# Four early blocks instead of two pass layer one twice: a quarter of its tiles first, the rest later

## The chip, the cores and the metric

The kernel runs on one core of a Trainium2 chip. The metric is the device time in microseconds of one execution. The engines are TensorE (PE), VectorE (DVE), ScalarE (ACT), GpSimdE (POOL) and SyncE (SP), which here issues every DMA.

## The reference

Attention over 4 batches, 8 heads, 576 positions and 64 columns a head, causal, with a linear memory beside it; then two dense layers over the 4 x 576 = 2304 rows of 512 columns:

```python
scores = scale * q @ k.T                      # causal, softmax
local = softmax(scores) @ v
q_p = elu(q) + 1
mem_out = (q_p @ M_prev) / (q_p @ z_prev + 1e-6)
x = sigmoid(beta) * mem_out + (1 - sigmoid(beta)) * local     # heads side by side: 2304 x 512
h = x @ w_in;  x = leaky_relu(h, 0.01) @ w_out                # layer one, 512 -> 2048 -> 512
h = x @ w_in2; out = (h - tanh(h)) @ w_out2                   # layer two
```

All values are float32. The kernel gets near float32 in the dense layers by splitting each operand into a high and a low part and adding three products (high x high, high x low, low x high).

## The kernel before

**Units and blocks.** A unit is one head pair of one batch. An A unit holds the first 256 queries and 256 keys; a B unit holds the other 320 queries (three query tiles) and all 576 keys. There are 16 A units (batch by batch, four head pairs each), then 16 B units. Four units make a block of 256 rows: blocks 0 to 3 from A, 4 to 7 from B; block 8 is gathered from the last 64 queries of each batch. A unit's steps (class Unit): load q, k, v and the memory (L444 to L481); the memory part, which takes phi of the raw queries and divides it by its norm on DVE and ACT (L490 to L531); its transposes (L539); the scores (L576, L581), masked and searched for their maximum on DVE (L602), exponentials on ACT (L622), scaling (L639, L641); transposes of the exponentials (L695), copied to SBUF (L397 and its neighbours); then memory and values into one PSUM tile o (L662, L717), and the copy of o into the block's x (fin, L730).

**Weights.** A weight arrives as the two 32-bit words of a 64-bit number. convert makes float32 of them and then the two parts: an absolute value on ACT (c_abs, L770), four steps on DVE (L773, L776, L781, L786), the high part (usually ACT, L393) and the low part (usually DVE, L406). Layer one has 32 such tiles of 128 x 512, 16 of either matrix. A pair p needs four of them. Layer two's weights are converted in 64 chunks, stored to DRAM, and loaded over layer one's when those are done with.

**Layer one.** layer1(n, p0, p1) passes block n over pairs p0 to p1 - 1, a sweep. It splits x into high and low halves (xs), does 24 up matmuls a pair (L835), the leaky ReLU (L892), the split of its result g, and 24 down matmuls a pair (L915) into two PSUM tiles dn. A sweep over part of the pairs stores dn as a partial sum (xps), and the later sweep loads it and adds it (L936). The order of the sweeps is SWEEPS (L387): blocks 0 and 1 over pairs 0 to 3, blocks 0 and 1 over pairs 4 to 7, and then blocks 2 to 8 over all eight.

**What sets the order.** The class Schedule is a planner that runs while the program is built. Each step has a priority, the engines it may go to with a time for each, the steps it needs and the buffers it takes. At every point of its own clock each free engine takes the first step by priority that is ready by the planner's times and has its buffers; the steps then stand in that fixed order in the engine's queue on the chip. Attention has priority (0, unit + offset), with offsets -1 for scores, 0 for loads, 0.3 for the memory part and 0.6 for values. A layer-one tile i has (0, 3.2 + 0.02 i) for the first 16 and (0, 7.2 + 0.02 i) for the rest. ACT, DVE and SP steps of layer one have (-1, n), ahead of everything; its matmuls have (1, ...), behind attention. RINGS (L33) gives the number of buffers of each tile; a ring's buffer comes free when all that use it are done. The two buffers of x hold a block's attention output until its last sweep has split it.

**Layer two** (L1093 to L1119) is written out by hand and follows when the planned part has ended.

Of the kernel before, what the change touches and what calls it, by code (L numbers as in the profile page):

```python
# [9 lines left out]
F32 = mybir.dt.float32  # L10
# [22 lines left out]
RINGS = {  # L33
# [3 lines left out]
}  # L37
# [195 lines left out]

W1_FROM, W1_STEP = (3.2, 7.2), 0.02

SPLIT = 2
W2_FROM, W2_STEP = 14, 0.25
# [3 lines left out]
def kernel(  # L241
# [42 lines left out]
    mask = const.tile([128, 512], BF16, name="mask")  # L284
    mask4 = const.tile([128, S], BF16, name="mask4")
    omg4 = const.tile([128, H // 2], F32, name="omg4")
# [20 lines left out]
    )  # L307
    nc.gpsimd.memset(mask4[:, 0:512], 0.0)
    for i in range(2):
        nc.vector.tensor_copy(out=mask4[64 * i:64 * i + 64, 512:S], in_=mask[0:64, 384:448])  # L310
    for m in mbs:
# [49 lines left out]

    x2s = [dram.tile([128, KT, 256], F32, name=f"x2s{n}") for n in range(NBLK)]
    xps = [dram.tile([128, KT, 256], F32, name=f"xps{n}") for n in range(SPLIT)]
    x8s = dram.tile([128, KT, 256], F32, name="x8s")
# [18 lines left out]
    x8_h = sc.new(None)  # L383
    x2_h = [sc.new(None) for n in range(NBLK)]
    xp_h = [[sc.new(None) for i in range(2)] for n in range(NBLK)]

    SWEEPS = [(n, h * NP // 2, (h + 1) * NP // 2) for h in range(2) for n in range(SPLIT)]  # L387
    SWEEPS += [(n, 0, NP) for n in range(SPLIT, NBLK)]
# [22 lines left out]
    class Unit:  # L411
# [14 lines left out]
        def declare(self, pr, prev):  # L426
            kind, b, hp = self.kind, self.b, self.hp
            nq, nk, nqc, nkc, q0 = self.nq, self.nk, self.nqc, self.nkc, self.q0
            n, nf = nqc + nkc, nq * 128
            op = lambda *a, **kw: sc.op(*a, prio=(pr[0], pr[1] + OFFSET[part_]), **kw)  # L430
            part_ = "load"
            new = sc.new
# [6 lines left out]

            qk, rq, zb, mb, v_ = new("qk"), new("rq"), new("zb"), new("mb"), new("v")  # L440
            n0 = 0 if kind == "A" else NA
# [25 lines left out]
            def load_v(e):  # L467
                v_.tile = att.tile([128, 2, 5, 64], F32, name="v", bufs=RINGS["v"])
                if kind == "B":
                    nc.sync.dma_start(  # L470
                        out=v_.tile, in_=v[b, 2 * hp:2 * hp + 2].rearrange("h (t p) d -> p h t d", p=128))
                    return
                for i, h in enumerate(heads):
                    nc.sync.dma_start(
                        out=v_.tile[:, i, 0:nk, :],
                        in_=v[b, h, 0:nk * 128, :].rearrange("(t p) d -> p t d", p=128))
# [68 lines left out]
            order["p"] = op([("pe", nq * 109 + 50)], tr_p, reads=[ph], alloc=[s, pT], after=in_order("p"))  # L545
            op(copies(nqc, True), p_out, reads=[s], writes=[pT], port=False)

# [5 lines left out]
            for tiles in ([[0, 1]] if kind == "A" else [[2], [3], [4]]):  # L553
                ss = [new("s"), new("s")]
                c0 = 0
                for t in tiles:
                    nn = min(S, (t + 1) * 128)
                    et[t - q0] = new(f"e{t if t > 1 else t + 2}")
                    made[t] = (ss, new("mx"), c0)
                    c0 += nn  # L560
# [27 lines left out]
            for i in range(nq):  # L588
# [7 lines left out]
                def maxi(e, j, t=t, ss=ss, ei=ei, mx=mx, nn=nn, half=half, c0=c0):  # L596
                    if t < 4:
                        out, in0, in1 = ei.tile[:, j, :], ss[j].tile[:, c0:c0 + nn], mask[:, 512 - nn:512]
                    else:
                        c = slice(j * half, (j + 1) * half)  # L600
                        out, in0, in1 = ei.tile[:, c], ss[j].tile[:, 0:half], mask4[:, c]
                    nc.vector.tensor_tensor_reduce(  # L602
                        out=out, in0=in0, in1=in1, scale=-scale,
                        scalar=mx.tile[:, 0:1] if t == 4 and j else BIG, op0=ALU.add, op1=ALU.min,
                        accum_out=mx.tile[:, j:j + 1])
# [7 lines left out]
                for j in range(2):  # L613
                    op([("dve", DVE(width))], lambda e, j=j, f=maxi: f(e, j), port=False,
                       reads=[ss[j]] + ([mx] if t == 4 and j else []), writes=[ei, mx])
# [51 lines left out]
            for kt in range(nk):  # L667
# [42 lines left out]
                for j in range(len(ss)):  # L710
                    op(copies(2 * w if len(ss) == 1 else w, True), lambda e, j=j, f=e_out: f(e, j), port=False,
                       reads=[ss[j]], writes=[pt])
# [17 lines left out]
            def fin(e):  # L730
                if xh.tile is None:
                    xh.tile = x_p.tile([128, KT, 320], F32, name="x")
                copy(e, xh.tile[:, hp, 0:nqc], o.tile[:, 0:nqc])

            op(copies(nqc, True), fin, reads=[o], writes=[xh], alloc=[xh] if first_x else [], port=False)
            if kind == "B":

                def rest(e):
                    nc.sync.dma_start(
                        out=x8s[:, hp, b * REST:(b + 1) * REST], in_=xh.tile[:, hp, 256:320])  # L740

                op([("sp", 500)], rest, reads=[xh], writes=[x8_h], lat=2300)

# [98 lines left out]
    def layer1(n, p0, p1):  # L842

        kind, b = blocks[n]
        sop = lambda *a, **kw: sc.op(*a, prio=(-1, n), **kw)
        if kind == "R":
            x = sc.new("x")

            def load_x(e):
                x.tile = x_p.tile([128, KT, 320], F32, name="x")  # L850
                nc.sync.dma_start(out=x.tile[:, :, 0:NA], in_=x8s)

            sop([("sp", 600)], load_x, reads=[x8_h], alloc=[x], lat=2600)
        else:
            x = x_h[kind, b]
        xs = sc.new("xs")

        def x_hi(e, i):
            if xs.tile is None:
                xs.tile = xs_p.tile([128, 2, KT, 256], F32R, name="xs")  # L860
            copy(e, xs.tile[:, 0, 2 * i:2 * i + 2], x.tile[:, 2 * i:2 * i + 2, 0:256])

        def x_lo(e, i):
            low(e, xs.tile[:, 1, 2 * i:2 * i + 2], x.tile[:, 2 * i:2 * i + 2, 0:256],
                xs.tile.bitcast(F32)[:, 0, 2 * i:2 * i + 2])

        for i in range(2):
            sop([("act", ACT(512)), ("dve", DVE(256))], lambda e, i=i: x_hi(e, i), reads=[x] + [xs] * i,
                writes=[xs], alloc=[] if i else [xs])
            sop([("dve", DVE(512))], lambda e, i=i: x_lo(e, i), reads=[x, xs], writes=[xs])  # L870
        dn = [sc.new("dn0"), sc.new("dn1")]
# [92 lines left out]
    for i, (m, f) in enumerate((m, f) for p in range(NP) for m in range(2) for f in (2 * p, 2 * p + 1)):  # L964
        firsts.append(convert(m, f, 0, 0, (0, W1_FROM[i // (2 * NP)] + i * W1_STEP), firsts[i - AHEAD:i - AHEAD + 1] if i >= AHEAD else ()))
    for i, (m, f, c) in enumerate(chunks):
# [197 lines left out]
```

## Time and profile before

| | us |
|---|---|
| median of 3 runs | 1095.72 (1094.59 to 1097.95) |
| profiled execution | 1094.87 |
| its span, first to last instruction | 1093.1 |
| PE busy | 1047.4 (96%) |
| DVE busy | 753.0 (69%) |
| ACT busy | 640.0 (59%) |
| POOL busy | 101.1 (9%) |

PE, DVE, ACT and POOL work side by side, so the busy times are not added. A PE row's end is modelled, and one row reaches into the next; the distance between the starts of two rows is the time that the first took. The granted clock is the share of TensorE's full rate. Times in a timeline are microseconds from the start of the span.

### The profile page before, as it was taken

The page shows a single profiled execution, that of the slowest core. Times are in us where ns is not written, and L with a number is a line of the kernel's source. Part 1 is how long each engine was busy: PE and PEld are TensorE (multiplying, and loading weights), DVE is VectorE, ACT ScalarE, POOL GpSimd, SP SyncE. Part 2 cuts the span into 40 slices and gives each one's busy share as a digit, 9 for nine tenths or more (in the row PEclk, how much of TensorE's full clock was granted, in tenths as well). Part 3 has the DMA queues.
Part 4 walks back from the last instruction along what each step waited for, and adds up shares of the span by engine and source line. Part 5 has one row for each costly group of instructions (what it writes and reads, how often), then busy time and mean ns, then how long its engine had stood idle before and what let it go on. Part 6 is the DMA issues. An engine that isn't in the chain of part 4 may idle for free.

```text
span 1093.1 us, 20334 instructions
## 1 busy us (share of the span) xinstructions
PE 1047.4 (96%) x7488; PEld 920.1 (84%) x7488; DVE 753.0 (69%) x2029; ACT 640.0 (59%) x1348; POOL 101.1 (9%) x103
## 2 busy tenths in 40 slices
PE   4796999999999999999999999999999999999997
PEld 2493987777887887788999999999999999999996
DVE  6999977878658748845222156777777777777774
ACT  5868576767547638635111023776667666676664
POOL 0000000000000000000000000122222222222221
PEclk8597899999999999999999999999999999999999
DMA  7857045656436426425000025201101101010000
GB/s 236 243 163 224 15 109 147 177 156 178 129 86 188 143 74 181 140 53 166 6 34 20 1 83 188 79 1 40 39 1 39 38 3 39 1 39 20 1 20 20
DMA packets 113906, 96.22 MB, mean 88 GB/s; under 512 B 63504, under 2 KB 92688, under 8 KB 113808
## 3 DMA queue, kind: packets, MB, share of 16 engines
q1 hardware_dynamic: 113808, 94.93, 29.5%
q8 instruction: 59, 0.97, 0.4%
q14 instruction: 39, 0.32, 0.1%
HBM read 75.50 MB, written 19.40 MB: 87 GB/s over the span
## 4 chain that ended last, share of the span: by engine, by line
PE 81%; DVE 7%; DMA 4%; ACT 4%; issue 1%; SPq 1%; ACTq 0%; DVEq 0%
PE up L835 34%; PE dn L1081 18%; PE dn L915 16%; PE s L695 4%; PE o L717 3%; PE s L576 3%; DMA w<-in_moe_w_out_dram 2%; DMA cv<-in_moe_w_in_dram 1%; PE o L662 1%; ACT e L622 1%; PE s L581 1%; DVE e L602 1%; DVE cv L786 1%; DVE w L406 1%; DVE cv L781 1%
## 5 line engine op out<-in xcount | busy, mean ns | idle before, releaser
L835 PE MATMUL up<-xs,w 128*128 128x256 f32 x3456 | 447.2, 284 | 2.1 <-ACT xs L393 1.1
L835 PEld LDWEIGHTS up<-xs,w 128*128 128x128 f32 x3456 | 431.1, 192 | 13.7 <-issue 5.8
L915 PE MATMUL dn<-gh,w 128*128 128x256 f32 x1152 | 161.3, 287 | 0.0
L915 PEld LDWEIGHTS dn<-gh,w 128*128 128x128 f32 x1152 | 146.5, 192 | 6.4 <-issue 5.7
L1081 PE MATMUL dn<-w,gh 128*128 128x512 f32 x576 | 144.2, 393 | 1.4 <-ACT gh L1068 1.3
L1058 DVE SCALAR_TENSOR_TENSOR gf<-u,w 128x512 f32<-128x512 f32 x72 | 86.3, 1199 | 81.9 <-ACT w L1055 81.9
L406 POOL TENSOR_TENSOR gl<-gf,gh 128x512 fp32r<-128x512 f32 x72 | 93.7, 1301 | 502.0 <-ACT gh L1068 502.0
L892 ACT ACTIVATE g<-up 128x512 f32<-128x512 f32 x72 | 42.7, 593 | 162.5 <-PE up L835 160.4
L1081 PEld LDWEIGHTS dn<-w,gh 128*128 128x128 f32 x576 | 103.3, 188 | 20.6 <-ACT gh L1068 2.1
L1050 ACT ACTIVATE u<-up 128x512 f32<-128x512 f32 x72 | 43.0, 597 | 116.3 <-PE up L835 116.3
L622 ACT ACTIVATE e<-e,mx 128x128 f32<-128x128 f32 (+4 forms) x144 | 82.6, 576 | 13.9 <-DVE mx L602 9.2
L395 DVE CAST gh<-g 128x512 fp32r<-128x512 f32 x39 | 16.7, 427 | 106.0 <-ACT g L892 105.9
L915 PE MATMUL dn<-gl,w 128*128 128x256 f32 x576 | 83.7, 286 | 0.0
L695 PE MATMUL s<-identr,e 128*128 128x128 f32 x448 | 68.3, 293 | 11.6 <-ACT e L639 5.0
L915 PEld LDWEIGHTS dn<-gl,w 128*128 128x128 f32 x576 | 74.9, 192 | 4.1 <-issue 3.9
L1081 PE MATMUL dn<-w,gl 128*128 128x512 f32 x288 | 77.0, 390 | 0.0
L695 PEld LDWEIGHTS s<-identr,e 128*128 128x128 f32 x448 | 52.6, 148 | 23.1 <-ACT e L639 8.2
L602 DVE CUSTOM_DVE_ANT_0 e<-s,mask 128x128 f32<-128x128 f32 (+4 forms) x144 | 64.0, 483 | 11.3 <-PE s L576 10.3
L393 ACT ACTIVATE pt<-s 128x320 f32<-128x320 f32 (+4 forms) x148 | 57.9, 437 | 18.9 <-PE s L683 12.8
L1081 PEld LDWEIGHTS dn<-w,gl 128*128 128x128 f32 x288 | 54.1, 188 | 11.2
L576 PE MATMUL s<-qk 64*128 64x128 f32 (+3 forms) x256 | 56.0, 524 | 5.3 <-DMA qk<-in_qkt_dram 4.5
L1061 DVE COPY_PREDICATED gf<-mk,up 128x512 f32<-128x512 int32 x72 | 53.7, 746 | 7.8 <-DVE up L1060 0.5
(92 smaller groups left out, 1316.5 us busy)
## 6 DMA issues: line engine op xcount, KB each, us to landing
w<-in_moe_w_in_dram SPq DMA_DIRECT2D x16, 512.0 KB, 5.2
w<-in_moe_w_out_dram SPq DMA_DIRECT2D x16, 512.0 KB, 4.8
cv<-in_moe_w_in_dram SPq DMA_DIRECT2D x32, 256.0 KB, 3.3
vs<-cv SPq DMA_DIRECT2D x64, 128.0 KB, 2.0
cv<-in_moe_w_out_dram SPq DMA_DIRECT2D x32, 256.0 KB, 3.1
v<-vs SPq DMA_DIRECT2D x32, 256.0 KB, 3.2
qk<-in_qkt_dram SPq DMA_DIRECT2D x16, 448.0 KB, 3.6
v<-in_v_dram SPq DMA_DIRECT2D x16, 320.0 KB, 3.4
```

The costliest lines, as they stand in the source:

```text
L393: nc.scalar.activation(out=out, in_=in_, func=AF.Copy)
L406: (nc.vector if e == "dve" else nc.gpsimd).tensor_tensor(out=out, in0=in_, in1=high, op=ALU.subtract)
L576: nc.tensor.matmul(ss[j].tile[:, c0:c0 + nn], lhsT=qk.tile[p, a:a + 128], rhs=qk.tile[p, kc:kc + nn], start=True, stop=True)
L602: nc.vector.tensor_tensor_reduce(out=out, in0=in0, in1=in1, scale=-scale, scalar=mx.tile[:, 0:1] if t == 4 and j else BIG, op0=ALU.add, op ...
L622: nc.scalar.activation(out=x, in_=x, func=AF.Exp, scale=-1.0, bias=mx.tile[:, k:k + 1], accum_out=sm.tile[:, j:j + 1])
L695: nc.tensor.transpose(ss[j].tile[:, a:a + 128], x, ident)
L835: nc.tensor.matmul(ps()[:, s, :], lhsT=w[:, wh * 512 + kt * 128:wh * 512 + (kt + 1) * 128], rhs=xs()[:, xh, kt, :], start=(kt == 0 and j = ...
L915: nc.tensor.matmul(dn[m // 2].tile[:, m % 2, :], lhsT=w[:, wh * 512 + m * 128:wh * 512 + (m + 1) * 128], rhs=gg.tile[:, s * 256:(s + 1) * ...
L1050: nc.scalar.activation(out=u, in_=h, func=AF.Square)
L1058: nc.vector.scalar_tensor_tensor(out=g, in0=u, scalar=lin, in1=w, op0=ALU.mult, op1=ALU.add)
L1061: nc.vector.copy_predicated(out=g, mask=mk.bitcast(I32), data=h)
L1081: nc.tensor.matmul(dn[t], lhsT=g[:, c0:c0 + 128], rhs=w[:, wh * 512:(wh + 1) * 512], start=(p == 0 and s == 0 and j == 0), stop=(p == NP - ...
```

## The change

SPLIT goes from 2 to 4, and CUT = 2 is new: blocks 0 to 3 pass pairs 0 and 1, then blocks 0 to 3 pass pairs 2 to 7, then blocks 4 to 8 pass all eight. The first 8 tiles' priority begins at 3.7, that of the other 24 at 15.7, with steps of 0.002. A first sweep stores its x to DRAM (xsv); the second loads it back in two halves, into buffers named e0 and e1. The A units of odd head pairs keep their exponentials in e0 and e1 too, so that two A units have buffers of their own. Raw queries get two buffers instead of one. A and B units' values are separate tiles, two buffers for A and one for B (before: two for both). The conversion of weights (cv) has three buffers instead of four. The x tile has 256 columns instead of 320: a B unit's last 64 columns are copied from o to a tile of their own (xr) and stored from there. Attention's copies out of PSUM and its maxima, which free a PSUM tile, get the priority (-0.5, unit + offset), ahead of every other attention step and of the conversions (free_op). The mask of the last query tile is kept for one half only, and the plain mask serves the other.

```diff
@@ -31,9 +31,9 @@
 RINGS = {
-    "qk": 2, "rq": 1, "zb": 2, "mb": 2, "v": 2, "ph": 1, "dnm": 2, "pT": 1, "mx": 6, "sm": 6,
-    "e2": 1, "e3": 1, "e4": 1, "s": 3, "o": 1, "pt": 4, "x": 2, "xs": 1,
-    "g": 2, "gl": 2, "gh": 2, "up": 2, "dn0": 1, "dn1": 1, "cv": 4, "v2": 4,
+    "qk": 2, "rq": 2, "xr": 1, "zb": 2, "mb": 2, "v": 1, "va": 2, "ph": 1, "dnm": 2, "pT": 1, "mx": 6, "sm": 6,
+    "e0": 1, "e1": 1, "e2": 1, "e3": 1, "e4": 1, "s": 3, "o": 1, "pt": 4, "x": 2, "xs": 1,
+    "g": 2, "gl": 2, "gh": 2, "up": 2, "dn0": 1, "dn1": 1, "cv": 3, "v2": 4,
 }
@@ -231,9 +231,11 @@
-W1_FROM, W1_STEP = (3.2, 7.2), 0.02
-SPLIT = 2
+W1_FROM, W1_STEP = (3.7, 15.7), 0.002
+SPLIT = 4
+CUT = 2
 W2_FROM, W2_STEP = 14, 0.25
@@ -282,7 +284,7 @@
     mask = const.tile([128, 512], BF16, name="mask")
-    mask4 = const.tile([128, S], BF16, name="mask4")
+    mask4 = const.tile([128, S // 2], BF16, name="mask4")
     omg4 = const.tile([128, H // 2], F32, name="omg4")
@@ -305,9 +307,9 @@
     )
-    nc.gpsimd.memset(mask4[:, 0:512], 0.0)
+    nc.gpsimd.memset(mask4[:, 0:S // 2 - 64], 0.0)
     for i in range(2):
-        nc.vector.tensor_copy(out=mask4[64 * i:64 * i + 64, 512:S], in_=mask[0:64, 384:448])
+        nc.vector.tensor_copy(out=mask4[64 * i:64 * i + 64, S // 2 - 64:S // 2], in_=mask[0:64, 384:448])
     for m in mbs:
@@ -360,6 +362,7 @@
     x2s = [dram.tile([128, KT, 256], F32, name=f"x2s{n}") for n in range(NBLK)]
+    xsv = [dram.tile([128, KT, 256], F32, name=f"xsv{n}") for n in range(SPLIT)]
     xps = [dram.tile([128, KT, 256], F32, name=f"xps{n}") for n in range(SPLIT)]
@@ -382,9 +385,10 @@
     x2_h = [sc.new(None) for n in range(NBLK)]
+    xv_h = [sc.new(None) for n in range(NBLK)]
     xp_h = [[sc.new(None) for i in range(2)] for n in range(NBLK)]
-    SWEEPS = [(n, h * NP // 2, (h + 1) * NP // 2) for h in range(2) for n in range(SPLIT)]
+    SWEEPS = [(n, 0, CUT) for n in range(SPLIT)] + [(n, CUT, NP) for n in range(SPLIT)]
     SWEEPS += [(n, 0, NP) for n in range(SPLIT, NBLK)]
@@ -428,6 +432,8 @@
             op = lambda *a, **kw: sc.op(*a, prio=(pr[0], pr[1] + OFFSET[part_]), **kw)
+            free_op = lambda *a, **kw: sc.op(*a, prio=(pr[0] - 0.5, pr[1] + OFFSET[part_]), **kw)
             part_ = "load"
@@ -437,7 +443,7 @@
-            qk, rq, zb, mb, v_ = new("qk"), new("rq"), new("zb"), new("mb"), new("v")
+            qk, rq, zb, mb, v_ = new("qk"), new("rq"), new("zb"), new("mb"), new("v" if kind == "B" else "va")
             n0 = 0 if kind == "A" else NA
@@ -465,14 +471,14 @@
             def load_v(e):
-                v_.tile = att.tile([128, 2, 5, 64], F32, name="v", bufs=RINGS["v"])
+                v_.tile = att.tile([128, 2, nk, 64], F32, name=v_.tag, bufs=RINGS[v_.tag])
                 if kind == "B":
...
                     nc.sync.dma_start(
-                        out=v_.tile[:, i, 0:nk, :],
+                        out=v_.tile[:, i],
                         in_=v[b, h, 0:nk * 128, :].rearrange("(t p) d -> p t d", p=128))
@@ -543,7 +549,7 @@
             order["p"] = op([("pe", nq * 109 + 50)], tr_p, reads=[ph], alloc=[s, pT], after=in_order("p"))
-            op(copies(nqc, True), p_out, reads=[s], writes=[pT], port=False)
+            free_op(copies(nqc, True), p_out, reads=[s], writes=[pT], port=False)
@@ -555,7 +561,7 @@
                     nn = min(S, (t + 1) * 128)
-                    et[t - q0] = new(f"e{t if t > 1 else t + 2}")
+                    et[t - q0] = new(f"e{t if t > 1 or self.hp % 2 else t + 2}")
                     made[t] = (ss, new("mx"), c0)
@@ -598,7 +604,7 @@
                         c = slice(j * half, (j + 1) * half)
-                        out, in0, in1 = ei.tile[:, c], ss[j].tile[:, 0:half], mask4[:, c]
+                        out, in0, in1 = ei.tile[:, c], ss[j].tile[:, 0:half], mask4 if j else mask[:, 0:half]
                     nc.vector.tensor_tensor_reduce(
@@ -611,7 +617,7 @@
                 for j in range(2):
-                    op([("dve", DVE(width))], lambda e, j=j, f=maxi: f(e, j), port=False,
+                    free_op([("dve", DVE(width))], lambda e, j=j, f=maxi: f(e, j), port=False,
                        reads=[ss[j]] + ([mx] if t == 4 and j else []), writes=[ei, mx])
@@ -708,7 +714,7 @@
                 for j in range(len(ss)):
-                    op(copies(2 * w if len(ss) == 1 else w, True), lambda e, j=j, f=e_out: f(e, j), port=False,
+                    free_op(copies(2 * w if len(ss) == 1 else w, True), lambda e, j=j, f=e_out: f(e, j), port=False,
                        reads=[ss[j]], writes=[pt])
@@ -729,17 +735,22 @@
                 if xh.tile is None:
-                    xh.tile = x_p.tile([128, KT, 320], F32, name="x")
-                copy(e, xh.tile[:, hp, 0:nqc], o.tile[:, 0:nqc])
-            op(copies(nqc, True), fin, reads=[o], writes=[xh], alloc=[xh] if first_x else [], port=False)
+                    xh.tile = x_p.tile([128, KT, 256], F32, name="x")
+                copy(e, xh.tile[:, hp], o.tile[:, 0:256])
+            free_op(copies(256, True), fin, reads=[o], writes=[xh], alloc=[xh] if first_x else [], port=False)
             if kind == "B":
+                xr = new("xr")
+                def fin_rest(e):
+                    xr.tile = att.tile([128, REST], F32, name="xr", bufs=RINGS["xr"])
+                    copy(e, xr.tile, o.tile[:, 256:320])
                 def rest(e):
-                    nc.sync.dma_start(
-                        out=x8s[:, hp, b * REST:(b + 1) * REST], in_=xh.tile[:, hp, 256:320])
-                op([("sp", 500)], rest, reads=[xh], writes=[x8_h], lat=2300)
+                    nc.sync.dma_start(out=x8s[:, hp, b * REST:(b + 1) * REST], in_=xr.tile)
+                free_op(copies(REST, True), fin_rest, reads=[o], alloc=[xr], port=False)
+                op([("sp", 500)], rest, reads=[xr], writes=[x8_h], lat=2300)
@@ -843,31 +854,53 @@
         sop = lambda *a, **kw: sc.op(*a, prio=(-1, n), **kw)
-        if kind == "R":
+        again = p0 > 0
+        if again:
+            halves = [sc.new("e0"), sc.new("e1")]
+            def load_half(e, i):
+                halves[i].tile = att.tile([128, 2, 256], F32, name=f"e{i}", bufs=1)
+                nc.sync.dma_start(out=halves[i].tile, in_=xsv[n][:, 2 * i:2 * i + 2])
+            for i in range(2):
+                sop([("sp", 600)], lambda e, i=i: load_half(e, i), reads=[xv_h[n]], alloc=[halves[i]], lat=2600)
+        elif kind == "R":
             x = sc.new("x")
             def load_x(e):
-                x.tile = x_p.tile([128, KT, 320], F32, name="x")
-                nc.sync.dma_start(out=x.tile[:, :, 0:NA], in_=x8s)
+                x.tile = x_p.tile([128, KT, 256], F32, name="x")
+                nc.sync.dma_start(out=x.tile, in_=x8s)
...
             x = x_h[kind, b]
+            if p1 < NP:
+                def save_x(e):
+                    nc.sync.dma_start(out=xsv[n], in_=x.tile)
+                sop([("sp", 600)], save_x, reads=[x], writes=[xv_h[n]], lat=2600)
         xs = sc.new("xs")
+        def x_half(i):
+            return halves[i].tile if again else x.tile[:, 2 * i:2 * i + 2]
...
                 xs.tile = xs_p.tile([128, 2, KT, 256], F32R, name="xs")
-            copy(e, xs.tile[:, 0, 2 * i:2 * i + 2], x.tile[:, 2 * i:2 * i + 2, 0:256])
+            copy(e, xs.tile[:, 0, 2 * i:2 * i + 2], x_half(i))
         def x_lo(e, i):
-            low(e, xs.tile[:, 1, 2 * i:2 * i + 2], x.tile[:, 2 * i:2 * i + 2, 0:256],
-                xs.tile.bitcast(F32)[:, 0, 2 * i:2 * i + 2])
+            low(e, xs.tile[:, 1, 2 * i:2 * i + 2], x_half(i), xs.tile.bitcast(F32)[:, 0, 2 * i:2 * i + 2])
         for i in range(2):
-            sop([("act", ACT(512)), ("dve", DVE(256))], lambda e, i=i: x_hi(e, i), reads=[x] + [xs] * i,
+            xi = halves[i] if again else x
+            sop([("act", ACT(512)), ("dve", DVE(256))], lambda e, i=i: x_hi(e, i), reads=[xi] + [xs] * i,
                 writes=[xs], alloc=[] if i else [xs])
-            sop([("dve", DVE(512))], lambda e, i=i: x_lo(e, i), reads=[x, xs], writes=[xs])
+            lo = sop([("dve", DVE(512))], lambda e, i=i: x_lo(e, i), reads=[xi, xs], writes=[xs])
+            if again:
+                att_ops.append(lo)
         dn = [sc.new("dn0"), sc.new("dn1")]
@@ -962,7 +995,7 @@
     for i, (m, f) in enumerate((m, f) for p in range(NP) for m in range(2) for f in (2 * p, 2 * p + 1)):
-        firsts.append(convert(m, f, 0, 0, (0, W1_FROM[i // (2 * NP)] + i * W1_STEP), firsts[i - AHEAD:i - AHEAD + 1] if i >= AHEAD else ()))
+        firsts.append(convert(m, f, 0, 0, (0, W1_FROM[i >= 4 * CUT] + i * W1_STEP), firsts[i - AHEAD:i - AHEAD + 1] if i >= AHEAD else ()))
     for i, (m, f, c) in enumerate(chunks):
```

## Rows read from the trace of the kernel before

**Rows 1.** The page's slices: PE's busy tenths in 40 equal slices of the span.

```profile
PE   4796999999999999999999999999999999999997
```

**Rows 2.** Stretches, us: busy time (instructions) of each engine, clock, DMA share, GB/s.

```profile
core 0: us, PE busy (x) PEld busy (x) DVE busy (x) ACT busy (x) POOL busy (x), PEclk, DMA share, GB/s
78.80:120.00 41.20, 30.95 (x166) 22.31 (x165) 39.92 (x139) 31.36 (x79) 0.74 (x2) 0.75 0.59 173
0.00:120.00 120.00, 86.28 (x470) 64.32 (x471) 107.47 (x386) 84.62 (x211) 2.96 (x13) 0.74 0.66 200
120.00:290.00 170.00, 167.87 (x1290) 135.85 (x1289) 140.02 (x605) 119.46 (x315) 3.11 (x9) 1.00 0.50 138
290.00:500.00 210.00, 207.57 (x1595) 171.51 (x1594) 142.27 (x538) 120.13 (x289) 1.37 (x9) 1.00 0.43 122
500.00:690.00 190.00, 190.00 (x1587) 188.76 (x1587) 73.07 (x136) 44.36 (x79) 0.00 (x0) 1.00 0.24 74
```

**Rows 3.** Groups by form, PE, 0 to 120 us: count, busy, mean ns, idle before.

```profile
L835 PE MATMUL up<-xs,w 128*128 128x256 f32 x144 | 23.3, 328 | 2.1 <-ACT xs L393 1.1 <-DVE xs L406 1.0
...
L576 PE MATMUL s<-qk 64*128 64x256 f32 x40 | 12.1, 590 | 0.0
...
L915 PE MATMUL dn<-gh,w 128*128 128x256 f32 x64 | 8.6, 285 | 0.0
...
L717 PE MATMUL o<-pt,v 128*64 128x256 f32 x32 | 7.9, 589 | 0.0
L915 PE MATMUL dn<-gl,w 128*128 128x256 f32 x32 | 4.5, 283 | 0.0
```

**Rows 4.** Timeline of PE, layer one: start, us, engine, line, tiles, count.

```profile
55.18 7.94 PE L835 MATMUL up<-xs,w 128*128 128x256 f32 x48
...
122.98 3.04 PE L835 MATMUL up<-xs,w 128*128 128x256 f32 x24
125.86 2.08 PE L915 MATMUL dn<-gh,w 128*128 128x256 f32 x16
...
128.74 3.04 PE L835 MATMUL up<-xs,w 128*128 128x256 f32 x24
```

**Rows 5.** Timeline of PE, 139 to 165 us: the steps of an A unit.

```profile
139.71 0.69 PE L662 MATMUL o<-pT,mb 128*128 128x256 f32 x2
...
160.33 0.82 PE L695 MATMUL s<-identr,e 128*128 128x128 f32 x6
...
161.78 0.93 PE L576 MATMUL s<-qk 64*128 64x128 f32 x8
...
162.98 0.38 PE L539 MATMUL s<-identr,ph 128*128 128x128 f32 x2
...
164.15 0.59 PE L662 MATMUL o<-pT,mb 128*128 128x256 f32 x2
164.68 0.87 PE L717 MATMUL o<-pt,v 128*64 128x256 f32 x8
```

**Rows 6.** DVE, a tile's low part: two starts, its group to 120 us, its whole range.

```profile
67.20 0.69 DVE L406 TENSOR_TENSOR w<-cv,w 128x512 fp32r<-128x512 f32 x1
...
69.67 0.69 DVE L406 TENSOR_TENSOR w<-cv,w 128x512 fp32r<-128x512 f32 x1
...
L406 DVE TENSOR_TENSOR w<-cv,w 128x512 fp32r<-128x512 f32 x27 | 18.5, 686 | 0.1
...
L406 DVE TENSOR_TENSOR w<-cv,w x32: 659/687/697, 22.9 to 134.2; 128x512 fp32r<-128x512 f32 x32
```

**Rows 7.** The chain that ended last, 8 to 24 us: start, us, what.

```profile
12.08 8.20 DMA w<-in_moe_w_out_dram
```

**Rows 8.** Timelines of ACT and DVE, 88 to 97 us: a tile's first and last step.

```profile
88.31 0.67 ACT L770 ACTIVATE cv<-w 128x512 f32<-128x512 f32 x1
...
95.23 0.69 DVE L406 TENSOR_TENSOR w<-cv,w 128x512 fp32r<-128x512 f32 x1
```

**Rows 9.** Groups by form, DVE and ACT, 112 to 290 us.

```profile
L936 DVE TENSOR_TENSOR g<-dn,g 128x512 f32<-128x512 f32 x4 | 2.7, 689 | 0.0
...
L393 ACT ACTIVATE pt<-s 128x128 f32<-128x128 f32 x6 | 1.7, 278 | 5.3 <-PE s L683 5.3
```

## The prediction

> **What bounds the kernel now.** I read the slices first. PE is full in nearly all of them; what it leaves open lies in the first four [rows 1]. The stretches say the same in microseconds: from 120 us on PE is busy 167.9 of 170 and 207.6 of 210, so whatever the change does there is worth only the 4.5 us that PE stood, unless it makes PE wait. Before 120 us PE is busy 86 us of 120, at a mean granted clock of 0.74, while DVE is busy 107.5 [rows 2]. So the kernel is bound by PE after 120 us and by DVE before, and the question is how much PE time is lost before PE fills.
>
> Lost PE time is the clock on the wall less the PE work done at the full level (2.4 GHz). A pair of layer-one tiles is 24 up and 24 down matmuls; run densely, one pair takes 128.74 - 122.98 = 5.76 us, 0.12 us a matmul [rows 4]. In the first 120 us there were 144 + 64 + 32 = 240 of them: 28.8 us. An A unit (one head pair of the first 256 queries of a batch) has PE rows of 0.82, 0.93, 0.38, 0.59 and 0.87 us; each reaches about 0.16 us into the next (a row of 24 ups lasts 3.04 us and the next begins after 2.88), so it is 3.6 - 0.8 = 2.8 us [rows 4, 5]. Eight A units were finished (32 value matmuls, 4 a unit) and two more had been scored (40 score matmuls, 4 a unit): 22.4 + 1.6 us [rows 3]. Together 52.8 us of work, so **some 67 us were lost by 120 us**, and next to nothing after.
>
> Why DVE is late: a tile of layer-one weights costs it five instructions, 69.67 - 67.20 = 2.47 us from one tile's last step to the next one's [rows 6]. 27 tiles by 120 us are 67 us; nine low parts of g and x (five and four, as long as a tile's own, 0.6 to the next) are 5.4. Of 107.5 that leaves 35 us for the constants at the start and 8.5 A units: at most 4.2 each. I take 3.8, with 3 for the constants [rows 2, 6]. So tiles give PE little for what they take: a first sweep over a pair buys 5.76 us of PE with about 10.5 us of DVE, an A unit 2.8 with 3.8, but a pair whose tiles are already there costs 0.6. The change moves the order towards the last kind.
>
> **What the change moves.** Before, 16 tiles come after three units and 16 more after seven, and two blocks pass four pairs each. After, 8 tiles come with unit 4, all four A blocks pass those two pairs, and 24 tiles come after unit 15 (or in holes before).
>
> First, units 0 to 3 and 8 tiles. DVE needs 3 + 4 x 3.8 + 8 x 2.47 = 38 us, plus the start (DVE idle 12.5 us in the first 120), so both pairs can run by about 50 us, much as before, where the first dense pair begins at 55.18 [rows 4]. The second buffer of raw queries lets unit 1's load leave before the weights; now ScalarE waits in order for a weight load that takes 8.2 us of the chain [rows 7]. I take nothing for it; between 0 and 5 us.
>
> Second, units 4 to 15 with eight pairs. Where PE is full, four A units pass from 139.71 to 164.15, 6.1 us each with filler [rows 5]; twelve take 73 us, and hold 12 x 2.8 + 7 x 5.76 = 74 us of PE. So PE is nearly full from about 50 to 122 us, where before, from 78.8 to 120, it was busy 31 of 41 us at a clock of 0.75 [rows 2]. DVE's spare time there goes to late tiles: by 122 us DVE has done 16 units (61), 8 low parts of g and 8 of x (10), constants 3, which with 15 us idle leaves 33 us: 13 tiles.
>
> Third, the other 19 tiles: 47 us, with six low parts of g, the split of block 0's reloaded x and the maxima of a B unit some 7 us more: until about **176 us**. PE's work by then: 16 A units (44.8), 13 pairs (75), scores of two B units and transposes of one: 128 us. (The last is an estimate from A's rows: a B unit has 2944 score columns where A has 768 in 0.77 us, so 2.95, and 22 transposes where A has 6 in 0.66, so 2.4; 8.3 in all.) Lost: 48 us. After that 18 pairs of blocks 1 to 3 lie ready, so PE should stay full. **67 - 48 = 19 us gained.** I take off two slow starts after thin stretches, for the 48 ups from 55.18 took 7.94 us instead of 48 x 0.12 + 0.16 = 5.9, so 2.0 each [rows 4]; and 3 us for waits in the longer mixed stretch, nearest to the 4.5 us in the 380 us after 120. **Gain 12 us.**
>
> Fourth, what is added. Two more sweeps split x again (two low parts of 0.69 each on DVE, the same number of high ones on ScalarE) and four more half blocks add the stored part: 4 x 0.69 [rows 9]. With four more copies of partial sums (0.6 each by the same length) and sixteen copies of 64 rest columns (no row of that shape: between 0 and the 0.28 of 128 columns, and I take 0.28) [rows 9] this is about 15 us on two engines, nearly all between 176 and 500 us, where DVE is busy 142 of 210 and ScalarE 120 [rows 2]: nothing on the path, 15 us if that cover were gone. On SP come 4 stores and 8 loads of x and 4 loads and 4 stores of partial sums. The reloads must land before a second sweep can split x: 0 if they are issued while the sweep before runs; bounded above by the 8.2 us of the worst load in the trace [rows 7], four times. I take 0: each half has its own buffer, free as soon as the sweep before has split it, and PE has that sweep's downs and B units meanwhile. One buffer of B's v: next v can be loaded only after the values matmul before it, half a B unit ahead; 0 to 8.2 us once, taken 0. The earlier turn for copies out of PSUM can win at most the 4.5 us of holes; taken 0. Layer two's weights are converted with three buffers instead of four and from 176 us instead of 134 [rows 6]. In the last stretch before layer two DVE is busy 73 of 190 us [rows 2], so that a delay of some tens of us finds room there; without that cover it would move the whole of layer two by its own length. I take 0.
>
> The profiled execution is 1094.87 us (span 1093.1, 1.8 around it), 0.85 below the median of the runs. 1094.9 - 12 = **1083 us**.
>
> **Rivals.**
>
> *A. More is hidden (1070 us).* If B attention fills the third stretch, since DVE can take a B step whenever a tile's next step is not ready yet, the 48 us lost shrink to the 36 or so lost up to 122 us: 12 us more. For it: B gives PE more per DVE time than a tile does. Against: the tiles' due time stands before nearly all of unit 16.
>
> *B. Three conversion buffers hold up the tiles (1096 us).* A tile holds its buffer from its absolute value to its low part. In the mixed stretch one ran from 88.31 to 95.92, 7.6 us [rows 8]. Three buffers let a tile through every third of that, 2.5 us: just what DVE needs. Beyond 7.4 us they bind. At 9.5 us between long B steps each of 19 tiles takes 0.7 us longer, 13 us in all: no gain left. Against it: where nothing but tiles runs, DVE itself sets their pace [rows 6].
>
> *C. PE works in cold bursts: slower (1103 us).* From 78.8 to 120 us, with waits between A units' steps, PE was busy 31 of 41 us at a clock of 0.75 [rows 2], and the dense run at 55.18 began slowly, 2.0 us lost [rows 4]. Now fourteen pairs stand in mixed stretches instead of dense runs. If each is begun like that, 14 x 2.0 = 28 us; I price ten, 20 us over my forecast. From six on the gain is gone. Place: the eight quarter pairs between 50 and 122 us, and block 0's six after it. Against: from 120 to 290 us A and B units alternate with pairs at a clock of 1.00 [rows 2]; once filler is there the clock holds. The Trainium skill (TensorE: Matmul & The Clock Gate, "HAM oscillation — how this bites in real kernels") says that an engine which waits between its bursts is throttled again and pays the change at every burst instead of once. The thin stretch before 120 us agrees (0.75), the mixed one after it shows no such falling back; by the rule taken to the end the sum would be rival C's, by the row of 120 to 290 us my forecast's.
>
> **Chances.** Forecast 0.50 (own range 1075 to 1091), A 0.13, B 0.17, C 0.20. The range reaches A's and most of C's: 1068 to 1103. A measurement here can tell about 0.3% (3.3 us) from no change: below 1092.4 is faster, above 1099.0 slower. Faster: the forecast, A and a little of B, 0.64; same 0.15; slower: C and a part of B, 0.21.
>
> **What would show it.** Right: the first pair's ups near 45 to 55 us; PE at 9 in the third and fourth slices; 16 A units done near 120 us; the last layer-one tile's low part near 176 us, not 134; DVE full until then; the lost PE time at that point near 50 us; layer two begun some 12 us sooner; no PE wait for the reloaded x. Wrong: DVE idle with tiles waiting for a buffer (B), a clock below 0.9 in slices three to six (C), PE waiting for reloads or v after 180 us, or A units slower than 7 us each, which would put the end of the tiles past 190 us and take 10 us or more of the gain.

## The result, and the profile after

The changed kernel takes 1085.03 us (median of 4 runs, 1082.97 to 1087.08) where the kernel before takes 1095.73 (1094.59 to 1097.95): a ratio of 0.9901, 95% interval 0.9883 to 0.9918. The profiled execution of the changed kernel is its fastest, 1082.97 us with a span of 1080.9; that of before had 1094.87 and 1093.1. So the spans differ by 12.2 us and the medians by 10.7.

The page's slices of the kernel after: PE's busy tenths and the granted clock in 40 equal parts of the span.

```profile
PE   5799999999999999999999999999999999999997
...
PEclk8699999999999999999999999999999999999999
```

PE now stands at 9 from the third slice on; before, the fourth was at 6, with a clock of 0.75 from 78.8 to 120 us [rows 1, 2]. The stretches of the kernel after, in the columns of [rows 2]:

```profile
0.00:50.00 50.00, 32.92 (x149) 20.98 (x150) 40.34 (x187) 37.23 (x112) 2.92 (x12) 0.78 0.83 243
50.00:80.00 30.00, 26.52 (x202) 20.76 (x201) 29.70 (x156) 27.21 (x82) 1.61 (x3) 0.98 0.65 189
80.00:120.00 40.00, 39.79 (x307) 31.23 (x304) 39.93 (x196) 36.86 (x110) 1.42 (x3) 1.00 0.73 212
120.00:176.00 56.00, 56.00 (x451) 52.03 (x450) 55.87 (x146) 41.38 (x83) 1.37 (x2) 1.00 0.52 165
176.00:290.00 114.00, 110.73 (x823) 85.93 (x823) 90.32 (x383) 76.36 (x189) 2.05 (x7) 1.00 0.60 166
290.00:500.00 210.00, 206.08 (x1590) 174.16 (x1589) 142.53 (x497) 110.15 (x269) 1.22 (x8) 1.00 0.46 135
```

From 80 to 176 us PE and DVE are both full, at a clock of 1.00. What PE still loses up to 176 us lies before 80 us.

PE's groups by form to 120 us (the answer to [rows 3]; two forms of the value matmuls, 4 of each a unit), then its layer-one groups to 176 us:

```profile
L846 PE MATMUL up<-xs,w 128*128 128x256 f32 x144 | 24.0, 314 | 1.4 <-ACT xs L397 1.0 <-DVE xs L410 0.2
...
L948 PE MATMUL dn<-gh,w 128*128 128x256 f32 x64 | 10.6, 296 | 0.0
L723 PE MATMUL o<-pt,va 128*64 128x256 f32 x56 | 10.6, 460 | 0.0
...
L948 PE MATMUL dn<-gl,w 128*128 128x256 f32 x32 | 5.7, 301 | 0.0
...
L846 PE MATMUL up<-xs,w 128*128 128x256 f32 x336 | 48.8, 297 | 1.4 <-ACT xs L397 1.0 <-DVE xs L410 0.2
L948 PE MATMUL dn<-gh,w 128*128 128x256 f32 x196 | 29.2, 290 | 0.0
L948 PE MATMUL dn<-gl,w 128*128 128x256 f32 x96 | 14.9, 289 | 0.0
```

By 120 us there are as many layer-one matmuls as before, 240, but 56 value matmuls where there were 32: **14 A units instead of 8**. The change put units where tiles were. The first ups, and the tiles' low parts, from the timelines of PE and DVE after (answers to [rows 4, 6]; one more low part is on POOL):

```profile
45.54 2.37 PE L846 MATMUL up<-xs,w 128*128 128x256 f32 x7 [1.00 <-ACT xs L397]
...
L410 DVE TENSOR_TENSOR w<-cv,w x31: 652/682/700, 23.9 to 172.5; 128x512 fp32r<-128x512 f32 x31
```

The last tile's step is at 172.5 us, 38 later than before, yet layer two begins earlier. Its first kind of down matmul, before 800 us, in the kernel before and in the kernel after (ns min/median/max, first and last start):

```profile
L1081 PE MATMUL dn<-w,gh x153: 389/390/506, 694.4 to 799.9; 128*128 128x512 f32 x153
```
```profile
L1114 PE MATMUL dn<-w,gh x177: 387/393/501, 675.6 to 799.9; 128*128 128x512 f32 x177
```

That is 18.8 us earlier, while the span ends only 12.2 earlier: **layer two itself became 6.6 us longer.** In 100 us of dense layer two PE makes fewer matmuls, before (first fence) and after (second):

```profile
700.00:800.00 100.00, 100.00 (x651) 91.21 (x650) 75.16 (x96) 69.84 (x117) 24.02 (x19) 1.00 0.06 22
```
```profile
690.00:790.00 100.00, 100.00 (x642) 91.07 (x641) 73.85 (x93) 68.08 (x114) 23.47 (x18) 1.00 0.07 22
```

PE is full and its clock 1.00 in both, and the code of layer two is the same. This is what the experiments began with.

### The profile page after: what moved, and what is told of

Read it like the earlier page. It is cut to its first block, busy times and chain, and to the rows that moved or that the text cites. A ratio compares the mean times of both kernels' runs of the same rounds, so it can differ in the third digit from the quotient of the medians.

```text
span 1080.9 us, 20416 instructions
## 1 busy us (share of the span) xinstructions
PE 1046.0 (97%) x7488; PEld 921.3 (85%) x7488; DVE 754.3 (70%) x2044; ACT 637.5 (59%) x1357; POOL 104.0 (10%) x107
## 4 chain that ended last, share of the span: by engine, by line
PE 77%; DVE 9%; DMA 6%; ACT 5%; issue 2%; SPq 1%; ACTq 0%; DVEq 0%
PE up L846 33%; PE dn L1114 18%; PE dn L948 14%; PE s L701 3%; PE s L582 3%; PE o L723 3%; DMA cv<-in_moe_w_out_dram 2%; DVE e L608 1%; PE o L668 1%; DVE cv L792 1%; DVE cv L797 1%; PE s L587 1%; ACT e L628 1%; DVE w L410 1%; DMA rq<-in_q_dram 1%
## 5 line engine op out<-in xcount | busy, mean ns | idle before, releaser
L846 PE MATMUL up<-xs,w 128*128 128x256 f32 x3456 | 454.4, 285 | 3.8 <-ACT g L925 2.4
L628 ACT ACTIVATE e<-e,mx 128x128 f32<-128x128 f32 (+4 forms) x144 | 82.7, 576 | 12.2 <-DVE mx L608 9.1
L399 DVE CAST gh<-g 128x512 fp32r<-128x512 f32 x32 | 13.6, 426 | 87.6 <-ACT g L925 87.6
L701 PE MATMUL s<-identr,e 128*128 128x128 f32 x448 | 64.7, 286 | 7.1 <-ACT e L645 5.2
L582 PE MATMUL s<-qk 64*128 64x256 f32 (+3 forms) x256 | 53.7, 497 | 9.7 <-DMA qk<-in_qkt_dram 7.0
L1085 DVE SCALAR_TENSOR_TENSOR hu<-up,u 128x512 f32<-128x512 f32 x72 | 49.6, 689 | 16.6 <-ACT u L1083 16.5
```

Of the source, the lines that this page charges most:

```text
L582: nc.tensor.matmul(ss[j].tile[:, c0:c0 + nn], lhsT=qk.tile[p, a:a + 128], rhs=qk.tile[p, kc:kc + nn], start=True, stop=True)
L628: nc.scalar.activation(out=x, in_=x, func=AF.Exp, scale=-1.0, bias=mx.tile[:, k:k + 1], accum_out=sm.tile[:, j:j + 1])
L701: nc.tensor.transpose(ss[j].tile[:, a:a + 128], x, ident)
L846: nc.tensor.matmul(ps()[:, s, :], lhsT=w[:, wh * 512 + kt * 128:wh * 512 + (kt + 1) * 128], rhs=xs()[:, xh, kt, :], start=(kt == 0 and j = ...
L1085: nc.vector.scalar_tensor_tensor(out=hu, in0=h, scalar=c4, in1=u, op0=ALU.mult, op1=ALU.mult)
```

## Experiments

Each is compared with its own runs of the kernel before. Those medians are 1094.25 to 1095.72, so times can be read side by side to about 1 us. The planner lays out the whole order anew for each edit of a step, a buffer or a priority, so such a run shows the edit together with the order that comes of it. The runs with other addresses alone keep the order.

**Where the tiles lie.** The half mask (576 instead of 1152 bytes a partition) moves all that is allocated behind it, weights included, down by 576 bytes; layer two's x, allocated from the other end, stays. The addresses in a partition, modulo 512, from the built programs, with the matmuls in 100 us of dense layer one and two from each trace:

```
                    w    x one  g one  x two  g two   layer one  layer two
before              448  448    448    480    448     836        651
after               384  384    384    480    384     835        642
before, half mask   384  384    384    480    384     836        637
pad 64              448  448    448    480    448     836        651
pad 64 and 32       448  480    480    480    448     859        651
pad 64 and 32, all  448  480    480    480    480     859        644
```

In other windows of these runs dense layer two has 650 to 652 where it has 651 here, and 636 to 643 where weights lie at 384.

Pad 64 bytes (`e1_pad64`):

```diff
-    mask4 = const.tile([128, S // 2], BF16, name="mask4")
+    mask4 = const.tile([128, S // 2 + 32], BF16, name="mask4")
```

> The changed kernel with 64 bytes a partition more for the mask of the last query tile, which nothing reads: the schedule is the same, all tiles behind the constants (the weights first) move up by 64 bytes and lie at 448 modulo 512 again, as before the change; layer two's split x stays where it was. Placement theory (the distance of the moving tile from the weights sets the pace of the matmuls): the 24 ups of a pair in layer two take 2.80 us from start to start as before the change, not 2.88, a pair 5.55 and not 5.64, so layer two is 6 to 7 us shorter and the time 1078 to 1079. Rival (the slower pace comes from the other engines or from the execution, not from addresses): no difference, 1085.

1076.46 us, ratio 0.982 (0.9798 to 0.9842), 8.6 below the kernel after. Layer two is back at 651 matmuls in 100 us. Its first down is at 672.7 and the span ends at 1071.2: 398.5 us, as before (398.7), against 405.3 after. That is 6.8 of the 8.6 us; layer two also begins 2.9 us earlier than after (675.6), which the pace of its matmuls does not explain and which stays open.

The mask alone in the kernel before (`e3_before_short_mask`):

```diff
-    mask4 = const.tile([128, S], BF16, name="mask4")
+    mask4 = const.tile([128, S // 2], BF16, name="mask4")
```

> The kernel before with only the mask of the last query tile halved, as the change has it; order, buffers and sweeps as before. All tiles behind it move down by 576 bytes. Placement theory: layer two's ups slow from 2.80 to 2.88 us for 24, its 72 pairs take 6 to 7 us longer, layer one is as before, the time 1102 to 1103. Rival without addresses: 1095.7.

1102.04 us, ratio 1.0067 (1.0047 to 1.0087). The timeline of layer two's downs, and its dense stretch:

```profile
L1081 PE MATMUL dn<-w,gh x96: 387/393/501, 694.0 to 757.9; 128*128 128x512 f32 x96
...
700.00:800.00 100.00, 100.00 (x637) 90.81 (x636) 73.63 (x94) 68.95 (x116) 23.60 (x19) 1.00 0.06 22
```

Layer two begins where it did before (694.0 and 694.4) and lasts 405.7 us instead of 398.7. A shorter mask alone costs 7 us of TensorE's pace; both directions show it.

A further 32 bytes ahead of layer one's x (`e2_pad64_32`), and the same kept open through layer two (`e5_pad_all`):

```diff
+    p1.enter_context(tc.tile_pool(name="pad", bufs=1)).tile([128, 8], F32, name="pad")
     x_p = p1.enter_context(tc.tile_pool(name="x", bufs=2))
```
```diff
+    ctx.enter_context(tc.tile_pool(name="pad", bufs=1)).tile([128, 8], F32, name="pad")
     p1 = ExitStack()
```

> As the run with 64 bytes, and 32 bytes more between the weights and layer one's tiles, so that layer one's x and g lie 32 bytes (modulo 512) from the weights' place, as layer two's x does from them in the kernel before; same schedule. Placement theory, if the distance alone decides: the 24 ups of a pair in layer one take 2.80 instead of 2.88 us, and its 24 downs the same, so up to 72 x 0.16 = 11.5 us less than with the 64 bytes alone where PE is full, some 1067 to 1070. If layer one's 0.12 us a matmul has another cause: as with the 64 bytes alone. Rival without addresses: 1085.

> The second pad now stays open through layer two, so that layer two's g lies 32 B beside its weights' residue (480 against 448, modulo 512) too, as x already does; before, and with the pad closed, it lay at 448 on 448. Placement theory, if the 32 B between the residues is itself what runs at 117 ns: nothing changes for the ups of layer two (already 117 ns), and the downs of layer two, if they were not at 117 yet, come down by up to 3 ns each: 864 downs in layer two x 3 = 2.6 us, so 1069 to 1072. If only the ups' operand matters: 1071.9 as with the pad closed, within 1. If the gain with the pad closed came from something else than layer one's placement, the same 1071.9, so this run tells only of the downs.

1071.92 (0.9793, 0.9773 to 0.9812) and 1072.63 (0.9794, 0.9777 to 0.9811). With x and g of layer one 32 bytes beside the weights, layer one goes from 836 to 859 matmuls in 100 us; the time falls by 4.5 us, less than expected. With layer two's g moved too, its pace falls from 651 to 644. The first kind of layer two's downs, before 760 us, without and with g moved:

```profile
L1115 PE MATMUL dn<-w,gh x136: 387/392/504, 667.5 to 758.0; 128*128 128x512 f32 x136
```
```profile
L1115 PE MATMUL dn<-w,gh x136: 392/396/498, 667.2 to 758.5; 128*128 128x512 f32 x136
```

So the address decides, but not by the distance alone: 32 bytes help x in both layers and g in layer one, and not g in layer two. One thing differs there: in layer two's downs the weights are the rhs operand and g is the lhsT; in the other matmuls of the two layers the weights are the lhsT. A rule by which rhs should lie 32 bytes above lhsT would fit these rows. No run tests it, and what the rule is stays open.

**Order or buffers.** The old sweeps and due times with the new buffers (`e4_old_sweeps`), and the new sweeps with one pair of exponential buffers for all A units (`e6_one_e`):

```diff
-W1_FROM, W1_STEP = (3.7, 15.7), 0.002
+W1_FROM, W1_STEP = (3.2, 7.2), 0.02
-SPLIT = 4
+SPLIT = 2
-CUT = 2
+CUT = 4
```
```diff
-                    et[t - q0] = new(f"e{t if t > 1 or self.hp % 2 else t + 2}")
+                    et[t - q0] = new(f"e{t if t > 1 else t + 2}")
```

> The changed kernel with the old order of sweeps and due times (two blocks in halves, tiles due at 3.2 and 7.2 with steps of 0.02); all its buffers, priorities and tiles stay. Order theory (the gain is that pairs whose tiles are there cost DVE little, so that sweeps and due times make it): the lost PE time is that of the kernel before, less what the second buffer of raw queries saves at the start (0 to 5 us); last tile near 130 us; layer two's first down at 690 to 694 us instead of 675.6; 1098 to 1104, with layer two's slower pace. Rival (the buffers of raw queries and exponentials make the gain, by letting A units overlap): first down near 676, 1085.

> All A units keep their exponentials in e2 and e3, as in the kernel before; e0 and e1 hold the reloaded halves alone. The sweeps and the tiles' order stay. If the new order of the sweeps makes the gain (my theory): an odd A unit now waits for the even one's exponentials to be transposed, which costs the mixed stretch 0 to 3 us, 1085 to 1089. If the second pair of buffers for A units makes it (rival): the loss of PE time before 120 us goes back to that of the kernel before, about 1094 to 1100.

1122.72 (1.0251, 1.0228 to 1.0274) and 1126.78 (1.0292, 1.0274 to 1.0311). Both are slower than either kernel, and neither theory had that. In the first, SP's timeline shows the loads of the reloaded halves:

```profile
169.44 0.34 SPq L864 DMA_DIRECT2D e<-xsv  x1
...
179.03 0.44 SPq L864 DMA_DIRECT2D e<-xsv  x1
```

The second sweeps cannot begin before them, although the blocks' x were stored at 51.0 and 100.2: the halves are to lie in e0 and e1, and those go to the odd A units first, to unit 15. In the second, PE's value matmuls and DVE's low parts to 120 us:

```profile
L723 PE MATMUL o<-pt,va 128*64 128x256 f32 x44 | 9.8, 538 | 0.0
...
L410 DVE TENSOR_TENSOR w<-cv,w 128x512 fp32r<-128x512 f32 x22 | 15.1, 686 | 0.1
```

11 units by 120 us instead of 14, and 22 low parts instead of 16. This fits the planner's rule: while a unit waits for its exponentials' buffer, DVE goes to tiles, whose pairs no sweep can use yet. It was not tried apart.

The kernel before with e0 and e1 for odd A units, room made by three conversion buffers and the half mask, padded (`e11_before_e01`):

```diff
-    "e2": 1, "e3": 1, "e4": 1, "s": 3,
+    "e0": 1, "e1": 1, "e2": 1, "e3": 1, "e4": 1, "s": 3,
-                    et[t - q0] = new(f"e{t if t > 1 else t + 2}")
+                    et[t - q0] = new(f"e{t if t > 1 or self.hp % 2 else t + 2}")
```

> The kernel before with A units of odd head pairs in exponential buffers of their own (e0, e1), three conversion buffers and the half mask (padded, so that the weights stay where they were modulo 512); its own sweeps and tile order. If the second pair of exponential buffers makes the gain alone (rival): A units pass in 7 us instead of 10 beside the tiles and the time falls to 1078 to 1088. If the new sweeps need the faster units and the faster units need the new sweeps (my theory after the two halves of the change each came out slower than both kernels): units wait for nothing but are not waited for by much, 1090 to 1097.

1117.11 (1.02, 1.0185 to 1.0215), again beyond both theories. Its stretch from 50 to 80 us and its first ups:

```profile
50.00:80.00 30.00, 7.46 (x29) 4.59 (x29) 30.00 (x88) 17.85 (x43) 1.00 (x2) 0.51 0.48 168
...
83.38 1.68 PE L835 MATMUL up<-xs,w 128*128 128x256 f32 x12
```

DVE is full of tiles and PE has 7.5 us of work in 30, as the first sweep starts at 83 us instead of 55 [rows 4]. Most of that is one wait. PE's transposes of exponentials from 40 to 80 us:

```profile
L695 PE MATMUL s<-identr,e 128*128 128x128 f32 x11 | 2.8, 396 | 27.5 <-DVE mx L602 26.6 <-ACT e L639 0.9
```

PE stands 26.6 us until DVE has taken maxima that the planner put behind a run of tile steps. Maxima are what the change's earlier turn moves ahead of the tiles, and this edit leaves that turn out. So the run shows that these buffers don't help the old kernel by themselves; what they are worth there with the earlier turn is not shown. (A conversion buffer fewer is part of this edit too; it wasn't tried apart.) No run of this group prices the order alone or the buffers alone: with the old sweeps the reloaded halves wait for unit 15, and here the earlier turn is missing. What they show is that in the changed kernel sweeps and exponential buffers need each other.

**The raw queries' second buffer** (`e7_one_rq`) and **the earlier turn** of the copies out of PSUM (`e12_no_free`):

```diff
-    "qk": 2, "rq": 2,
+    "qk": 2, "rq": 1,
```
```diff
-            free_op = lambda *a, **kw: sc.op(*a, prio=(pr[0] - 0.5, pr[1] + OFFSET[part_]), **kw)
+            free_op = lambda *a, **kw: sc.op(*a, prio=(pr[0], pr[1] + OFFSET[part_]), **kw)
```

> One buffer of raw queries instead of two. As predicted (0 to 5 us): 1085 to 1090. If the second buffer is what lets three units begin before the weights' loads (rival): the first units' memory part falls behind by a weight load of 8 us and the kernel with it, 1092 to 1094.

> The copies out of PSUM and the maxima get attention's usual priority again instead of the earlier turn. As predicted (at most the holes of 4.5 us): 1083 to 1090. If the earlier turn is what lets A units pass at 7 us beside the tiles (rival): PSUM tiles stay taken while a tile's DVE steps run, units go back to 10 us, 1100 or more.

1096.82 (1.0016, 1.0003 to 1.0028) and 1087.68 (0.9927, 0.9913 to 0.9942). One buffer of raw queries costs 11.8 us, the whole gain, and more than even the rival gave it. The waits of those who use the raw queries, to 120 us, after and with one buffer (us, times), and its value matmuls:

```profile
  DMA rq<-in_q_dram: 1.0, 1
```
```profile
  DMA rq<-in_q_dram: 6.3, 3
...
L723 PE MATMUL o<-pt,va 128*64 128x256 f32 x48 | 9.7, 490 | 0.0
```

12 units instead of 14. The earlier turn is worth 2.7 us, within what was expected.

**Is DVE's work the limit?** Less of it (`e9_no_max`), and two conversion buffers (`e8_cv2`):

```diff
-        op([("dve", DVE(n / 2))], c_max, reads=[g], writes=[g])
+        if layer:
+            op([("dve", DVE(n / 2))], c_max, reads=[g], writes=[g])
```
```diff
-    "g": 2, "gl": 2, "gh": 2, "up": 2, "dn0": 1, "dn1": 1, "cv": 3, "v2": 4,
+    "g": 2, "gl": 2, "gh": 2, "up": 2, "dn0": 1, "dn1": 1, "cv": 2, "v2": 4,
```

> Leaves out of the computation the maximum with a tiny number in the conversion of layer one's 32 weight tiles (a DVE step of 0.34 us each); nothing else. If DVE sets the end of the tiles, as I predicted: 32 x 0.34 = 10.7 us of DVE gone, the last tile's low part near 162 us instead of 172.5, and the kernel about 9 to 11 us faster, 1074 to 1076. If PE is what is full from 80 us on and DVE only fills its holes: only the 8 early tiles' 2.7 us count, 1081 to 1084.

> Two conversion buffers instead of three. My theory (DVE's own work sets the tiles' pace, three buffers do not bind): a tile that holds its buffer for 5 to 7.6 us lets one through every 2.5 to 3.8 us with two; at the upper end each of 24 late tiles takes up to 1.3 us longer, so 0 to 20 us slower, nearest 10: 1095. If three buffers bind already (rival B of the prediction): two buffers cost a third of the stretch of 54 us and more, 20 us at least: 1105 or above. Same time as with three (1085, within 3): the ring has slack to spare.

1084.57 (0.9905, 0.989 to 0.992) and 1077.48 (0.9838, 0.9821 to 0.9855). With 10.7 us less of DVE's work the last low part is 8 us earlier and the time the same: PE's end was not set by it.

```profile
L410 DVE TENSOR_TENSOR w<-cv,w x31: 659/685/692, 23.7 to 164.3; 128x512 fp32r<-128x512 f32 x31
```

Two buffers made the kernel faster by 7.5 us; I had every theory on the other side. PE's and DVE's groups to 120 us, and the stretch behind the tiles:

```profile
L723 PE MATMUL o<-pt,va 128*64 128x256 f32 x60 | 11.8, 478 | 0.0
...
L410 DVE TENSOR_TENSOR w<-cv,w 128x512 fp32r<-128x512 f32 x14 | 9.6, 683 | 0.2 <-ACT w L397 0.2
...
176.00:290.00 114.00, 113.55 (x857) 88.81 (x852) 88.42 (x383) 78.37 (x193) 0.92 (x6) 1.00 0.52 143
```

15 units and 14 low parts: holding tiles back lets units pass, as I read it, and from 176 to 290 us PE stands 0.4 us instead of 3.3.

**Both together** (`e10_best`: both pads of the run at 1071.92, and two conversion buffers):

> Both pads (weights at 448, layer one's x and g at 480, as in the run at 1071.9) and two conversion buffers instead of three. If the two gains are independent (placement 13 us, two conversion buffers 7.5): 1071.9 - 7.5 = 1064 to 1066. If the gain of two buffers came from where the tiles lay instead of the order: 1072, as with three.

1065.2 us (1062.86 to 1066.35), ratio 0.9726 (0.9713 to 0.9739): the gains of placement and of two buffers add up, and this version beats both kernels, the changed one by 19.8 us.

## Why the prediction came out

Predicted 1083 us, measured 1085.03. The size was met, and part of the reason for it was luck.

- **Lost PE time, 67 down to 48 by 176 us: held in total, not in its parts.** To 176 us there are 628 layer-one matmuls (75.4 us by the prediction's 0.12), 16 A units (44.8), two B units scored and one transposed (8.3): 128.5, so 47.5 lost. The last low part came at 172.5 (176 predicted). But by 120 us some 46 were lost, not 36, and in the third stretch under 2, not 12. A units took 127 us, not 122; 14 were done by 120.
- **The 7 us taken off the gross gain of 19: failed, in the 4 for two slow starts.** The 3 for waits came nearly whole: PE stands 7.2 us from 176 to 500, 6.8 of them named waits, against 4.5 after 120 us before. With these 2.7 off, 67 - 47.5 = 19.5 us leave 16.8; layer two began 18.8 us earlier. So no slow start took anything more, and 2 us came on top that my sum doesn't explain. The clock was below 1.00 only before 80 us (0.78 to 50 us, 0.98 from there), where the sum of lost time holds every slow start already; I took them off a second time.
- **A term was missing:** the half mask, for which my sum had nothing, moved the weights and cost layer two 6.6 us. It took the place of the 4 by chance; without it the kernel is at 1076.5, 8.6 us lower, 6.8 of them in layer two.
- **"DVE before, PE after": half right.** DVE is full to 176 us, but taking 10.7 us off it gave 0.5. What PE lacks early is blocks of x, thus finished A units; their number by 120 us is 8 before, 14 after, 15 with two conversion buffers. This is a reading, not shown: with the maximum left out there were 15 as well, but PE stood 4.5 us between 120 and 176, and the runs at 1126.78 and 1096.82 us had 11 and 12, more than the kernel before.
- **The second buffer of raw queries at 0, between 0 and 5 us: failed**; 11.8. I took it for a matter of one load at the start, but with one buffer the units fall behind for good: 12 by 120 us instead of 14. The named waits for these loads are only 6.3 us against 1.0, so how one buffer comes to cost 11.8 is not shown in full. The second pair of exponential buffers had no price at all in the sum: 6.1 us a unit came from a stretch where few tiles stood between a unit's steps [rows 5]. Without them the kernel is 42 us slower.
- **The earlier turn, reloads, B's v, the added sweeps at nothing: held** where tried (2.7 us for the first) or seen. PE's waits from 176 us to layer two name no reloaded x; the largest:

```profile
PE up L846 <- ACT g L925: 2.4, 2, 2.0
PE s L582 <- ACT pt L397: 1.8, 1, 1.8
PE s L701 <- DVE e L647: 0.8, 1, 0.8
```

- **Rival A** came true in its place, the third stretch filled, but the second one gave it back. **Rival B** was wrong in sign: fewer conversion buffers help. **Rival C** did not come: the granted clock is 0.98 from 50 to 80 us and 1.00 after.

## What to carry to other kernels

Taking away a buffer that several small units share can cost more than the whole change gains (11.8 and 42 us here, against 10.7): price it by the pace of the units, and try each with and without. Where a planner lays out the order, look for one long wait before a variant's time is put down to the part that was left out: 26.6 us of PE hung on a few maxima. Before crediting a change with a time, compare the pace of a stretch that the change doesn't touch; if that moved, look at where its operands lie. A planner that fills each hole can fill it with work that nobody needs yet, so a smaller ring can be the better order.

## What the runs showed of the hardware that was not expected

TensorE's dense pace depends on where its operands lie in a partition. At a clock of 1.00 and with PE full, layer two made 650 to 652 matmuls in 100 us with weights and g at 448 and x at 480 (modulo 512), 644 with g at 480 too, and 636 to 643 with weights and g at 384; layer one 836 with x and g at the weights' residue and 859 with them 32 bytes beside it. The two pads together took 13 us off the kernel: 1085.03 against 1071.92.
